# Weights written to SBUF as bf16 by casting transfers of GpSimd, without staging and casts, with another order table

## The chip, the cores and the metric

The kernel runs on one core of a Trainium2 chip. The metric is the device time of one execution in microseconds (us). Executions of one kernel spread by about 1% to either side here, so medians of several runs are given. A ratio is the mean time of one kernel's fast runs over that of the kernel before in the same rounds on the same chip, with a 95% interval, so it is not quite the ratio of the medians quoted beside it. A run over 1.5% above the fastest of the same kernel counts as slow; medians are over all runs, ratios over fast ones alone, and all profiles shown are of fast runs.

The engines are called PE or TensorE (matmuls; PEld its weight loads), DVE or VectorE, ACT or ScalarE, POOL or GpSimd, and SP or SyncE, which here only issues transfers. Operands lie in SBUF and the results of matmuls in PSUM, both memories on the chip. A staging buffer is a place in SBUF where float32 data lands before an engine casts it to bf16.

## The reference, cut to what matters

Sliding-window attention (a query sees keys at a distance up to 32) over 8 batches, 8 heads, 576 positions of 64 values; then a feed-forward part with a 3-tap convolution along the sequence and a sigmoid gate. Input and output are float32.

```python
scores = q @ k.T / 8;  scores[abs(i - j) > 32] = -1e9
x = softmax(scores) @ v                       # 8 x 576 x 512 after joining the heads
h = maximum(x @ w_in, 0)                      # w_in 512 x 1024
c = conv_w[0]*h[s-1] + conv_w[1]*h[s] + conv_w[2]*h[s+1]
out = (h * sigmoid(c)) @ w_out                # w_out 1024 x 512
```

## The kernel before

The kernel is one list of operations. A table, ORDER, gives the order in which they are emitted, the engine of each and its buffers; each engine, SyncE's queue included, runs its share strictly in that order. A token is the number of an operation, a letter (P TensorE, V VectorE, S ScalarE, G GpSimd, D a transfer issued by SyncE, Q one issued by ScalarE, F a matmul on zeros) and buffer numbers.

```python
BUFS = {'st': 3, 'qkb': 5, 'qkT': 3, 'attn': 2, 'rec': 4, 'xn': 3, 'hT0': 8, 'hT1': 6, 'hT2': 6, 'cp': 2, 'gT': 4, 'y': 7}
...
    class InOrder:                        # every engine keeps the order of the table
        def __getattr__(self, name):
            do = getattr(self.engine, name)
            return lambda *args, **kwargs: fixed(do(*args, **kwargs))
...
    def load_v(b, c):                     # v of batch b, block c of 128 keys: rows of 64 floats, 256 bytes each
        ...
            loader[e].dma_start(vst[s0 - lo:s1 - lo, c, :, :], v[b, :, s0:s1, :].rearrange("h p d -> p h d"))
    def shift_v(b, c0, c1):               # vo: v moved by 64 keys, from the bf16 copy ve
        op(f"vo hi {b} {c0} {c1}", lambda e: copy(e, vo[0:64, c0:c1], ve[64:128, c0:c1]), ...)
...
    def load_w(which, i):                 # half a weight, 1 MB of float32, into a buffer of the ring "st"
        s = w_slot[which, i] = Slot(ring)
        ...                               # issued by SyncE (D in the table)
                loader[e].dma_start(
                    flat[:, 0:KC * n].rearrange("p (c f) -> p c f", c=KC),
                    moe_w_in.rearrange("(c p) f -> p c f", p=128)[:, :, n * i:n * i + n])
    def cast_w(which, m):                 # 16 casts, on ScalarE, GpSimd and VectorE
                copy(e, w_in_sb[:, :, 128 * m:128 * m + 128], src[:, :, 128 * (m % n):128 * (m % n) + 128])
```

The ring st holds q and k as they arrive and, in between, the weights. vst holds one float32 batch of v, block by block: the next batch's block can land only when this batch's block has been cast to ve.

The softmax here doesn't subtract the row's maximum and nothing guards it: scores larger than these inputs give would overflow.

## Time and profile before

| | before |
|---|---|
| median, range | 227.55 us, 226.43 to 228.67 (2 runs) |
| span of the profiled run | 225.6 us |
| columns that the real matmuls must stream | 194.2 us |
| first matmul on w_in | 25.80 us |
| TensorE's loss before it / after it | 18.6 / 8.9 us |

"Loss" is the length of a stretch less the columns of the real matmuls that start in it, at one column per 1/2.4 ns. (The prediction adds rounded stretches to 9.1 us; 221.7 - 194.2 - 18.6 is 8.9.) The lines of the page, of the stretches and of the chain stand in the prediction.

### The profile page before, as it was taken

Reading aid. Unit: us, or ns where it says so; the run is one execution under the profiler, and the core shown is the slowest. Engines: PE = TensorE matmul, PEld = TensorE weight load, DVE = VectorE, ACT = ScalarE, POOL = GpSimd, SP = SyncE. Lnnn points to the kernel's source line nnn. Section 1 sums busy time; section 2 is a strip of 40 time slices with the busy share of each in tenths; the row PEclk is TensorE's granted clock in tenths of the full one; section 3 lists DMA queues with packets and bytes.
Section 4 is the critical chain, followed back from the end, with each engine's and each line's share of the span. In section 5 each row is a group of like instructions: output and inputs, shape, how many; then the busy total and the mean of one; then the engine's idle time right before and its main releaser. Section 6 shows DMA issues by size and latency. Waiting matters only on the chain.

```text
span 225.6 us, 7189 instructions
## 1 busy us (share of the span) xinstructions
PE 211.5 (94%) x2720; PEld 122.9 (54%) x2720; DVE 197.3 (87%) x467; ACT 187.5 (83%) x474; POOL 137.7 (61%) x203
## 2 busy tenths in 40 slices
PE   7698899989989999989999998999999999999993
PEld 5366567658555655545555454545655565455541
DVE  6279869899999979797999788989999999899990
ACT  2689899998989889879889989689989999777642
POOL 5978654654376937695368736756386735566640
PEclk9889999999999999999999999999999999999999
DMA  6999999999989999999997989994535212501224
GB/s 201 331 285 358 355 266 281 321 308 253 290 170 324 317 175 287 236 306 224 288 347 129 202 278 358 182 231 147 144 36 118 99 46 49 175 1 49 93 101 178
DMA packets 66391, 48.16 MB, mean 214 GB/s; under 512 B 50781, under 2 KB 50805, under 8 KB 66357
## 3 DMA queue, kind: packets, MB, share of 16 engines
q1 hardware_dynamic: 64992, 46.32, 78.6%
q10 hardware_dynamic: 1364, 1.39, 2.9%
q8 instruction: 21, 0.34, 0.8%
q14 instruction: 14, 0.11, 0.2%
HBM read 32.52 MB, written 9.44 MB: 186 GB/s over the span
## 4 chain that ended last, share of the span: by engine, by line
PE 41%; DVE 18%; ACT 17%; DMA 13%; issue 5%; SPq 3%; POOL 2%; DVEq 0%; ACTq 0%; POOLq 0%
PE pf L232 41%; DMA st<-in_k_dram 7%; ACT attn L232 6%; DVE pf L232 5%; DVE gT L232 4%; SPq L232 3%; DMA out_dram<-y 3%; ACT xn L232 3%; DVE qkT L232 2%; ACT pf L232 2%; DMA vo<-ve 2%; DVE attn L232 2%; DVE xn L232 2%; ACT qkb L232 2%; ACT y L232 1%
## 5 line engine op out<-in xcount | busy, mean ns | idle before, releaser
L232 PE MATMUL pf<-xT,w_in_sb 128*128 128x385 bf16 (+2 forms) x416 | 73.4, 315 | 3.6 <-ACT hT L232 0.9
L232 PE MATMUL pf<-w_out_sb,gT 128*128 128x512 bf16 x288 | 72.2, 380 | 0.0
L232 POOL TENSOR_SCALAR cp<-hT,conv_w_sb 128x384 f32<-128x384 bf16 (+1 forms) x63 | 38.9, 622 | 46.1 <-ACT hT L232 20.2
L232 ACT ACTIVATE pf<-pf 128x384 f32<-128x384 f32 (+1 forms) x104 | 48.2, 477 | 13.1 <-DVE pf L232 11.1
L232 DVE SCALAR_TENSOR_TENSOR gT<-pf,hT 128x384 bf16<-128x384 f32 (+1 forms) x104 | 52.1, 517 | 5.5 <-ACT pf L232 5.1
L232 PEld LDWEIGHTS <-w_in_sb 128*128 128x128 bf16 x416 | 38.6, 98 | 27.8 <-issue 4.5
L232 ACT ACTIVATE attn<-pf 128x512 bf16<-128x512 f32 (+1 forms) x96 | 41.4, 522 | 1.8 <-PE pf L232 1.8
L232 ACT ACTIVATE hT<-pf 128x385 bf16<-128x385 f32 (+2 forms) x76 | 35.4, 487 | 6.0 <-PE pf L232 5.6
L232 PEld LDWEIGHTS <-gT 128*128 128x128 bf16 x288 | 26.0, 98 | 25.7 <-DVE gT L232 0.5
L232 DVE SCALAR_TENSOR_TENSOR pf<-hT,conv_w_sb,pf 128x384 f32<-128x384 bf16 (+1 forms) x61 | 34.7, 586 | 1.2 <-PE pf L232 1.1
L232 PE MATMUL pf<-hT,diag_w 128*128 128x384 bf16 (+1 forms) x153 | 30.9, 309 | 0.9 <-DVE xn L232 0.6
L232 POOL TENSOR_SCALAR qkb<-st 128x1152 bf16<-128x1152 f32 (+1 forms) x23 | 25.7, 1122 | 7.6 <-DMA st<-in_k_dram 3.2
L232 DVE COPY qkT<-pf 128x576 bf16<-128x576 bf16 x35 | 25.6, 750 | 4.9 <-PE pf L232 4.9
L232 POOL TENSOR_TENSOR cp<-cp,cp 128x384 f32<-128x384 f32 (+1 forms) x24 | 24.4, 1016 | 1.6
L232 DVE TENSOR_TENSOR attn<-attn,mask 128x1152 bf16<-128x1152 bf16 x26 | 23.0, 886 | 2.4 <-ACT attn L232 2.3
L232 ACT ACTIVATE xn<-pf,rec 128x64 bf16<-128x64 f32 x96 | 22.0, 360 | 1.5 <-DVE rec L232 1.5
L232 ACT COPY y<-pf 128x512 f32<-128x512 f32 x30 | 18.1, 605 | 3.9 <-PE pf L232 3.7
L232 DVE SCALAR_TENSOR_TENSOR pf<-hT,conv_w_sb,cp 128x384 f32<-128x384 bf16 (+1 forms) x35 | 21.2, 618 | 0.0
L232 POOL TENSOR_TENSOR attn<-attn,mask 128x1152 bf16<-128x1152 bf16 x6 | 14.2, 2371 | 8.4 <-ACT attn L232 8.4
L232 DVE TENSOR_TENSOR xn<-pf,rec 128x256 bf16<-128x256 f32 x48 | 18.9, 410 | 0.0
L232 ACT COPY qkT<-pf 128x576 bf16<-128x576 bf16 x29 | 18.6, 664 | 0.4 <-PE pf L232 0.2
L232 PEld LDWEIGHTS <-diag_w 128*128 128x128 bf16 x153 | 13.3, 97 | 9.8 <-issue 1.3
(49 smaller groups left out, 235.2 us busy)
## 6 DMA issues: line engine op xcount, KB each, us to landing
st<-in_q_dram SPq DMA_DIRECT2D x16, 576.0 KB, 6.8
out_dram<-y SPq DMA_DIRECT2D x36, 256.0 KB, 3.8
st<-in_k_dram SPq DMA_DIRECT2D x14, 576.0 KB, 8.2
vst<-in_v_dram SPq DMA_DIRECT2D x24, 256.0 KB, 7.0
vst<-in_v_dram SPq DMA_DIRECT2D x15, 192.0 KB, 5.7
vo<-ve SPq DMA_DIRECT2D x11, 260.0 KB, 5.6
st<-in_moe_w_in_dram SPq DMA_DIRECT2D x2, 1024.0 KB, 9.3
st<-in_moe_w_out_dram SPq DMA_DIRECT2D x2, 1024.0 KB, 9.4
```

Source lines behind the costliest of these rows:

```text
L232: return lambda *args, **kwargs: fixed(do(*args, **kwargs))
```

## The change

Its intent is to take 16 casts, the staging and its waits away: GpSimd can issue a transfer that converts float32 to bf16 on the way. The rest of the table was made anew for it. The core of the diff (cuts marked; the table, the choice of convolution ways and small index changes are left out):

```diff
-BUFS = {'st': 3, 'qkb': 5, 'qkT': 3, 'attn': 2, 'rec': 4, 'xn': 3, 'hT0': 8, 'hT1': 6, 'hT2': 6, 'cp': 2, 'gT': 4, 'y': 7}
+BUFS = {'st': 3, 'qkb': 4, 'qkT': 3, 'attn': 2, 'rec': 8, 'xn': 2, 'hT0': 9, 'hT1': 7, 'hT2': 7, 'cp': 8, 'gT': 3, 'y': 6}
+MASKS = ('ma', 'mm', 'mm', 'mm', 'mm', 'mm', 'mm', 'am')   # 'a': the mask is added on TensorE
 ...
     def load_w(which, i):
-        s = w_slot[which, i] = Slot(ring)
 ...
-                loader[e].dma_start(
-                    flat[:, 0:KC * n].rearrange("p (c f) -> p c f", c=KC),
+                gpsimd.dma_start(
+                    w_in_sb[:, :, n * i:n * i + n],
 ...
-    def cast_w(which, m):
 ...
-        op(f"cast w_{which} {m}", emit, reads=[("wst", which, m // n)], writes=[("w_" + which, m)], use=[s])
```

In the new table both w_in transfers stand near the front of GpSimd's list, and both w_out transfers behind the first shifts of v. SyncE's order is different too: q and k of both halves of batch 0 come before v block 2.

## The prediction

> **What bounds the kernel now.** I read the engine shares first, then the slices, then cut the span into stages with the view of busy time by stretch, and only then the chain of waits. The page of the kernel before, engine shares and slices (each digit a fortieth of the span, in tenths):
>
> ```profile
> PE 211.5 (94%) x2720; PEld 122.9 (54%) x2720; DVE 197.3 (87%) x467; ACT 187.5 (83%) x474; POOL 137.7 (61%) x203
> ...
> PE   7698899989989999989999998999999999999993
> DVE  6279869899999979797999788989999999899990
> ACT  2689899998989889879889989689989999777642
> ...
> DMA  6999999999989999999997989994535212501224
> ```
>
> TensorE is busy 94% of the span, but two things flatter that: 75 matmuls on a tile of zeros (13.5 us in the list of groups) only keep its clock up, and the end of a matmul is modelled. So I counted what it must do, from the starts and shapes of the matmuls in the trace: all real matmuls stream 194.2 us worth of columns at one column per 1/2.4 ns. The median step between two like matmuls of 512 columns is 216 ns against 213 ns of columns, so this rate is reached. The busy time by stretch (columns: length, then PE, weight loads, DVE, ACT, POOL, clock, DMA share, GB/s):
>
> ```profile
> 0.00:25.80 25.80, 21.13 (x329) 14.52 (x329) 17.43 (x56) 18.53 (x46) 19.67 (x65) 0.93 0.98 298
> 25.80:51.40 25.60, 24.82 (x354) 16.24 (x355) 21.85 (x56) 24.43 (x67) 14.39 (x20) 1.00 1.14 303
> 51.40:103.50 52.10, 49.71 (x808) 29.88 (x805) 48.10 (x115) 45.35 (x112) 34.08 (x34) 1.00 1.07 256
> 103.50:136.20 32.70, 30.87 (x410) 17.10 (x403) 28.87 (x68) 29.71 (x77) 19.04 (x23) 1.00 1.04 257
> 136.20:184.50 48.30, 48.25 (x604) 26.52 (x604) 47.05 (x103) 42.48 (x108) 31.50 (x37) 1.00 0.64 152
> 184.50:221.70 37.20, 36.70 (x228) 18.64 (x226) 33.95 (x74) 26.32 (x67) 19.04 (x26) 1.00 0.24 79
> ```
>
> Against these lengths the columns of real matmuls that start in each stretch are 7.2, 23.9, 49.0, 30.0, 48.3 and 35.7 us. TensorE therefore loses 18.6 us before its first matmul on w_in, then 1.7, 3.1, 2.7, 0.0 and 1.6: 9.1 us in all the rest. The final copy and store add 225.6 - 221.7 = 3.9. So a new order has 9.1 us to win in the middle, plus whatever the start yields; 48 us of the span cannot move. The chain of waits (start, length, what) says who costs these losses:
>
> ```profile
> 1.83 6.50 DMA st<-in_k_dram
> ...
> 16.40 2.95 ACT attn L232 x7
> ...
> 25.80 7.68 PE pf L232 x93
> ...
> 35.45 0.63 ACT w_out_sb L232
> ...
> 38.64 0.50 ACT w_out_sb L232
> 39.14 0.18 ACT attn L232
> 39.32 0.21 ACT w_out_sb L232
> ...
> 136.25 48.21 PE pf L232 x603
> ```
>
> The start is a load, then ScalarE (busy 12.40 of the 12.5 us from 12.5 to 25). From 33.5 to 51 the chain is all ScalarE, with w_out casts on it: 0.63 + 0.50 + 0.21 = 1.34 us. From 51 to 75 it is VectorE. From 136 on TensorE alone.
>
> **What the skill says.** "DMA: Bandwidth & Descriptors", SWDGE vs HWDGE vs iDMA: a transfer that casts must be issued by GpSimd, whose cores write its descriptors; its Latency and other measured facts put first byte at about 1 us against 0.6. No GpSimd transfer is in the trace of before, so this is untested here. The same page, Issuing engines are not separate DMA queues: all queues share the 16 engines. This trace has the DMA share at 0.98 in the first 25.8 us, so an added early transfer takes from the others. "SBUF — State Buffer", Who interferes with whom, says GpSimd is blocked while a VectorE copy uses both ports; descriptors could be late by one VectorE copy, 0.4 to 0.8 us here. "TensorE: Matmul & The Clock Gate", What's actually happening: an idle array runs at half clock. The granted clock here is 0.89 in the first 12.5 us, with 75 zero matmuls to hold it, and 1.00 from 25 on; the page and the trace agree.
>
> **The change, part by part.** (1) Casts of the weights go:
>
> ```profile
> L232 POOL TENSOR_SCALAR w_in_sb<-st 128x512 bf16<-128x512 f32 x4 | 3.3, 836 | 0.6 <-DMA st<-in_moe_w_in_dram 0.5
> L232 ACT CAST w_in_sb<-st 128x512 bf16<-128x512 f32 x4 | 2.6, 771 | 0.0
> L232 ACT CAST w_out_sb<-st 128x512 bf16<-128x512 f32 x4 | 2.5, 621 | 0.0
> L232 POOL TENSOR_SCALAR w_out_sb<-st 128x512 bf16<-128x512 f32 x3 | 1.8, 617 | 3.6 <-DMA st<-in_moe_w_out_dram 3.6
> ```
>
> ScalarE loses 5.1 us (4 x 0.771 = 3.1 and 4 x 0.621 = 2.5 as single durations), POOL 5.1, DVE 0.5. On a path: the 1.34 us shown, and about 1.5 us of the w_in casts on ScalarE, which stand between the exponentials and the normalisation of batch 0 (19.3 to 23.2). In exchange POOL writes four sets of descriptors, an estimate of 4 x 1 us from the skill's 1 us.
>
> (2) The two w_in transfers stand first on POOL after its memsets, with no wait. The memsets end at 2.8 us before; the changed kernel adds seven small ones (affine selects took 0.24 us each), so I expect issue at 4 to 5 us, while k of the first batch lands at 8.4 and its second half at about 12.5. SP now issues q and k of both halves ahead of most of v (0.26 MB, 0.9 us at 298 GB/s earlier). If 2 MB of w_in takes half of the engines from 6 us on, the remaining 1.4 MB at 150 GB/s lands at about 15, 2.5 us later than now. From that landing to the first w_in matmul is 25.8 - 12.5 = 13.3 us now; less 1.5 (casts) and about 1.3 (part 3). 15 + 10.5 = 25.5: the start is a draw, -2 to +3.
>
> (3) Batch 0's second half and batch 7's first are masked by adding -30000 on TensorE: 8 matmuls of 512 columns and 4 of 128, 8 x 0.213 + 4 x 0.053 = 1.9 us more; four VectorE multiplies of 886 ns go, 3.5 us. In batch 0 the exponential then leads straight to the value matmuls: one to two multiplies (0.76 each at 19.4 and 20.9) off the starting chain, so 1.3.
>
> (4) The new tables. Comparing the two programs' instructions: zero matmuls 75 to 16 (none before the second half of batch 0's scores); turning matmuls 58 to 44 (14 x 0.053 = -0.7); taps on TensorE 118 to 123 of 384 and 35 to 24 of 192 (+0.8 - 0.9). With part 3, TensorE has 194.2 + 1.1 = 195.3 us of columns. VectorE, with the durations of before: 18 fewer qkT copies (-13.5), 22 fewer PSUM taps (-13.5), masks -3.5, more casts and copies: about -10 us. ScalarE: 18 more qkT copies (+12.0) against 5.6 of weight casts, 6.3 of q and k casts, 3.6 of y: about -4. POOL: 10 more sums (1.03 each), 14 more 384-column products (0.62 each), with the rest about +17, to 155, still the least busy. cp goes from 2 buffers to 8, rec 4 to 8, hT one more of each; xn 3 to 2, gT 4 to 3, y 7 to 6, qkb 5 to 4.
>
> The sum from the profiled 225.6: start 0; middle, 9.1 us of losses cut by some 4.5 (1.34 from w_out casts; the VectorE stretch from 51 to 75 shorter; products waiting for a cp buffer, 17.0 us of POOL waits on DVE in the table of waits, mostly off the path); TensorE work +1.1; end 0. That is -3.4, or 222 in the profile. The plain time is 227.55 beside it, so some 224. I go 1.7 us lower, to 222.3, by choice: an order table that comes with a change was presumably searched until it paid, and that belief, not a profile line, is the reason.
>
> **Rivals.** The start gets worse: w_in collides with q and k, and without zero matmuls TensorE is cold. For it: DMA share 0.98, clock 0.93 even with them. Against: half speed costs only about 0.5 us per batch of 18 to 36 small matmuls (0.44 to 1.14 us each at full speed), and w_in was needed before the same first matmul anyway. It would make 226 to 229. Second rival: TensorE is the bound and the casts were hidden; only the 1.1 us of new columns show, 227 to 229. For it: the 48 us stretch without loss. Against: ScalarE and VectorE saturated from 33 to 75. Third: fewer buffers of xn, gT and qkb make new waits on loads and batches, taking back what the casts gave: 224 to 227. Fourth, a good one: the losses of the middle fall under 3 us and the start gains 2: 217 to 219.
>
> **Range and chances.** The best case and the bad start give 217 and 227.5 as the eight-in-ten range. Two per cent is 4.55 us, so the border lies at 223.0, just above my number: faster 0.53, same 0.41, slower 0.06.
>
> **What would show it.** First w_in matmul at 24 to 28 us; k of batch 0's second half landing near 15; clock below 0.9 in the first 25 us; a POOL-issued queue of 4 MB read; ScalarE near 183 and VectorE near 187 us busy; the stretches between first w_in matmul and 136 us losing 4 instead of 7.5 us. I am wrong if the first w_in matmul comes after 29 us, if w_out lands so late that the first w_out matmuls wait, or if the middle loses as much as before.

## More of the kernel before

One more view is needed for later: what SyncE issued between 23 and 37 us, from its timeline (start and length in us; the length is that of issuing).

```profile
23.34 0.37 SPq L232 DMA_DIRECT2D st<-in_moe_w_out_dram  x1
23.76 3.51 SPq L232 DMA_DIRECT2D vst<-in_v_dram  x2
27.39 4.15 SPq L232 DMA_DIRECT2D st<-in_moe_w_out_dram  x1
31.58 5.42 SPq L232 DMA_DIRECT2D vst<-in_v_dram  x4
```

SyncE's queue never stands still here: weights and small v blocks follow one another in one queue.

## The result, and the profile after

238.20 us (237.87 to 238.53, 2 runs) against 227.55: ratio 1.047 [1.038, 1.057], slower. The range of the prediction ended at 227.5.

The page of the changed kernel, engine shares and slices in tenths:

```profile
PE 205.2 (87%) x2653; PEld 116.8 (49%) x2653; DVE 199.6 (84%) x462; ACT 185.1 (78%) x474; POOL 160.5 (68%) x224
...
PE   1325796897999999999999899989999999999992
...
PEclk9999999999999999999999999999999999999998
DMA  6999989956898999999999989999503712430324
```

PE is thin up to about 59 us (ten slices of 5.9 us) and full after that. DMA dips to 5 and 6 in slices 9 and 10, where it was full before. The clock line reads full from the start, but that is no measurement: this trace has no record of the clock before 23.37 us, and the view prints a stretch without a record as full. The matmuls tell otherwise. The first 18 small turning matmuls of the attention, in the changed kernel and, at a clock recorded as full, before:

```profile
6.45 0.84 PE L233 MATMUL pf<-ident,qkb 64*128 64x64 bf16 x18 [1.21 <-DVE qkb L233]
```

```profile
7.09 0.44 PE L232 MATMUL pf<-ident,qkb 64*128 64x64 bf16 x18 [0.48 <-POOL qkb L232]
```

So without the zero matmuls TensorE ran at about half speed here. (Before, too: its first clock record is at 6.29 us, and up to then its zero matmuls of 256 columns started 213 ns apart, against 109 ns at full clock. The 0.89 that the prediction reads for the first 12.5 us is therefore too high.) Busy time by stretch (columns as in the prediction; the clock of 1.00 in the first line is the missing record):

```profile
0.00:31.35 31.35, 13.55 (x276) 9.23 (x277) 19.81 (x67) 14.21 (x32) 19.23 (x63) 1.00 0.95 241
31.35:62.50 31.15, 26.18 (x375) 16.25 (x377) 23.56 (x59) 25.84 (x72) 12.04 (x17) 1.00 0.82 181
62.50:103.00 40.50, 39.25 (x598) 23.43 (x596) 37.38 (x92) 36.37 (x98) 29.45 (x31) 1.00 1.02 273
```

The first stretch ends at the first matmul on w_in, 31.35 us. Counted as before, TensorE loses 23.1 us in the first stretch (18.6 before), 7.1 in the second (1.7 before, up to 51.4), and 6.5 in all the rest up to 232.0 (7.2 before). The columns are 195.3 us (+1.1), the tail 4.4 (3.9). So 4.5 + 5.4 - 0.7 + 1.1 + 0.5 = 10.8 us, the whole difference between the two spans: 9.9 of it are waits in the first 62 us, and the later table loses even 0.7 us less. The chain of waits says what made it (start, length, what):

```profile
3.37 15.02 DMA vst<-in_v_dram
18.41 0.63 ACT ve L233
...
20.81 2.56 DVE diag_w L233 x6
...
31.20 0.35 DVE ve L233
31.57 0.47 SPq L233
...
32.13 8.20 DMA vst<-in_v_dram
```

There are two barriers, that is, waits for a load behind which the engines come to stand, one after the other. **The first**: v block 2 of batch 0 is issued at 3.37 us and lands at 18.38, after 15.0 us. Before, it was issued at 2.34 and landed at 9.36. ScalarE waits 4.09 us for it, in its fixed order, while other work stands behind; VectorE and TensorE follow. w_in had been issued at 4.44 and 5.39 and landed at 14.70 and 18.06, long before its first use at 31.35. With w_in moved away and SyncE's order kept (x2 below) the same block landed at 12.41. So of the 9.0 us by which it is later than before, about 3 come from its new place behind q and k of the second half, and about 6 from w_in beside it. **The second**: SyncE is idle for 8 us. Its timeline, to be laid beside the one of before:

```profile
22.55 0.90 SPq L233 DMA_DIRECT2D st<-in_k_dram  x1
31.57 0.47 SPq L233 DMA_DIRECT2D vo<-ve  x1
32.13 9.44 SPq L233 DMA_DIRECT2D vst<-in_v_dram  x5
```

The shift vo<-ve waits for a VectorE cast that ends at 31.5, and the v block behind it, which has nothing to do with that cast, is issued only at 32.13. It then takes 8.2 us, because GpSimd's two w_out transfers (issued at 29.12 and 29.91) are in the same 16 DMA engines. VectorE waits for it with relu and gate behind.

Why so long for a small block? In the trace a v block is some 64 packets of 256 bytes on each DMA engine, 20 to 23 ns each: 1.4 us of work. The Trainium skill, "DMA: Bandwidth & Descriptors", Queues, rings and completion order, says that an engine goes round robin between the queue rows it has work for. The first barrier agrees: from 12 to 16 us 609 packets of v and 603 of GpSimd's casting packets (1024 bytes written) started, of 31 and 96 ns on average. At one for one, 64 x (31 + 96) ns is 8.1 us, an estimate from these durations; the packets of v run from 9.7 us, and the block landed at 18.38. (The page speaks of turns of some 9 to 17 descriptors; these counts cannot tell turns of one record from turns of several.)

The second barrier is not the same. Between 30.71 and 36.14 us no packet of SyncE's queue started at all, only GpSimd's, although the shift had been issued at 31.57 and the v block at 32.13; v's own packets then took from about 37.2 to 40.4 us. Why SyncE's queue stood still there is not shown. Before, weights and v stood in one queue, where a v block waits only for what was issued ahead of it.

### The profile page after: what moved, and what is told of

Its sections match the earlier page's. It is cut to its first block, busy times and chain, and to the rows that moved or that the text cites. A ratio compares the mean times of both kernels' runs of the same rounds, so it can differ in the third digit from the quotient of the medians.

```text
span 236.4 us, 7025 instructions
## 1 busy us (share of the span) xinstructions
PE 205.2 (87%) x2653; PEld 116.8 (49%) x2653; DVE 199.6 (84%) x462; ACT 185.1 (78%) x474; POOL 160.5 (68%) x224
## 4 chain that ended last, share of the span: by engine, by line
PE 35%; DVE 28%; DMA 12%; POOL 9%; ACT 7%; issue 5%; SPq 2%; DVEq 0%; ACTq 0%; POOLq 0%
PE pf L233 35%; DMA vst<-in_v_dram 10%; DVE pf L233 9%; POOL cp L233 6%; DVE gT L233 5%; ACT attn L233 3%; DMA xT<-xn 2%; DVE hT L233 2%; DVE qkT L233 2%; ACT pf L233 2%; DVE xn L233 2%; SPq L233 2%; DVE attn L233 1%; DVE y L233 1%; DVE diag_w L233 1%
## 5 line engine op out<-in xcount | busy, mean ns | idle before, releaser
L233 POOL TENSOR_SCALAR cp<-hT,conv_w_sb 128x384 f32<-128x384 bf16 (+1 forms) x84 | 58.5, 706 | 33.2 <-DVE hT L233 17.1
L233 ACT ACTIVATE pf<-pf 128x384 f32<-128x384 f32 (+1 forms) x104 | 46.4, 468 | 13.5 <-DVE pf L233 9.8
L233 PEld LDWEIGHTS <-w_in_sb 128*128 128x128 bf16 x416 | 38.2, 98 | 25.9 <-issue 3.2
L233 POOL TENSOR_TENSOR cp<-cp,cp 128x384 f32<-128x384 f32 (+1 forms) x37 | 36.2, 985 | 1.3
L233 ACT COPY qkT<-pf 128x576 bf16<-128x576 bf16 x47 | 28.9, 657 | 9.5 <-PE pf L233 9.3
L233 ACT ACTIVATE hT<-pf 128x385 bf16<-128x385 f32 (+2 forms) x72 | 32.7, 485 | 4.6 <-PE pf L233 2.9
L233 PE MATMUL pf<-hT,diag_w 128*128 128x384 bf16 (+1 forms) x147 | 30.7, 313 | 4.1 <-DVE hT L233 3.2
L233 DVE SCALAR_TENSOR_TENSOR pf<-hT,conv_w_sb,cp 128x384 f32<-128x384 bf16 (+1 forms) x41 | 29.3, 728 | 3.1 <-POOL cp L233 2.6
L233 DVE SCALAR_TENSOR_TENSOR pf<-hT,conv_w_sb,pf 128x384 f32<-128x384 bf16 (+1 forms) x40 | 22.7, 571 | 4.5 <-PE pf L233 4.3
L233 PE MATMUL pf<-ident,qkb 64*128 64x64 bf16 x576 | 15.1, 196 | 10.2 <-ACT qkb L233 5.2
L233 POOL TENSOR_SCALAR qkb<-st 128x1152 bf16<-128x1152 f32 (+1 forms) x18 | 21.5, 1203 | 2.7 <-DMA st<-in_q_dram 1.4
L233 DVE TENSOR_TENSOR attn<-attn,mask 128x1152 bf16<-128x1152 bf16 x22 | 20.4, 925 | 0.1
L233 PEld LDWEIGHTS <-qkb 64*128 64x128 bf16 x576 | 11.2, 98 | 17.1 <-DVE qkb L233 9.1
```

## The experiments

Eighteen runs were made, in five rounds. Milestones below are from one profile each: "w_in" is the first matmul on w_in, "gate n" the start of the n-th gate operation on VectorE. Profiles of kernels that share an order up to some point differ there by up to 1.6 us, so a single milestone is no finer than that.

| run | median us | ratio [95%] | w_in | gate 4 | gate 12 | gate 32 |
|---|---|---|---|---|---|---|
| before | 227.55 | | 25.8 | 32.7 | 46.7 | 83.1 |
| after | 238.20 | 1.047 [1.038, 1.057] | 31.4 | 43.9 | 56.0 | 92.9 |
| x1_old_order_cast_dma | 233.31 | 1.024 [1.015, 1.033] | 26.4 | 33.6 | 47.4 | 85.3 |
| x2_w_in_later | 240.31 | 1.056 [1.051, 1.062] | 29.1 | 44.0 | 57.4 | 94.4 |
| x3_v_earlier | 240.44 | 1.058 [1.050, 1.067] | 31.1 | 44.1 | 58.3 | 95.2 |
| x6_zero_matmuls | 240.04 | 1.056 [1.050, 1.062] | 32.6 | 44.3 | 56.3 | 93.3 |
| x7_vo_on_vector | 236.83 | 1.034 [1.025, 1.043] | 30.9 | 40.5 | 52.6 | 89.5 |
| x4_w_out_later | 238.85 | 1.046 [1.036, 1.055] | 30.7 | 40.4 | 53.0 | 89.9 |
| x5_all_four | 234.06 | 1.021 [1.014, 1.028] | 28.7 | 38.3 | 52.3 | 89.4 |
| x9_w_from_scalar | 234.29 | 1.019 [1.009, 1.029] | 30.5 | 37.6 | 51.4 | 88.0 |
| x10_no_casts (wrong) | 230.62 | 1.008 [1.001, 1.014] | 26.0 | 32.9 | 46.4 | 86.0 |
| x11_only_w_out | 228.14 | 1.005 [0.998, 1.013] | 25.1 | 32.0 | 45.8 | 83.6 |
| x13_batch1_first | 233.50 | 1.026 [1.022, 1.030] | 28.5 | 38.5 | 50.5 | 87.6 |
| x15_diag_on_gpsimd | 232.90 | 1.025 [1.020, 1.030] | 27.8 | 37.8 | 49.8 | 86.7 |
| x16_batch3_first | 233.77 | 1.027 [1.021, 1.033] | 28.2 | 39.3 | 51.4 | 88.3 |
| x17_half_weights_after (wrong) | 233.28 | 1.027 [1.021, 1.033] | 29.1 | 38.7 | 50.8 | 87.7 |
| x18_half_weights_before (wrong) | 234.43 | 1.030 [1.024, 1.036] | 26.1 | 33.0 | 48.9 | 85.6 |
| x19_stores_later | 227.79 | 1.002 [0.996, 1.008] | 26.2 | 33.1 | 47.0 | 82.6 |
| x20_v_before_products | 232.24 | 1.021 [1.013, 1.028] | 28.6 | 39.3 | 50.1 | 87.0 |
| x21_w_out_and_stores | 228.69 | 1.004 [0.997, 1.011] | 25.9 | 32.8 | 46.7 | 83.5 |

Edits of the table are written with the names of the operations.

### Round one: which part of the change, and the start

**x1_old_order_cast_dma**: the old table and buffers; only the way of the weights is new.

```diff
 # old table; at the places of SyncE's weight loads
-  loader[e].dma_start(flat..., moe_w_in...)    # SyncE, into the ring
+  gpsimd.dma_start(w_in_sb..., moe_w_in...)    # casting, and the same for w_out
   cast_w: emit nothing
```

> The headline part alone: the order table of before, with w_in and w_out written as bf16 by casting transfers from GpSimd at the places where SP loaded them, and no weight casts. If casting transfers cost time by themselves (descriptors, slower transfers, shared engines), this is slower than before, 229 to 233 us. If what cost 10.7 us was where the transfers and loads stand in the new order, this is as fast as before or 1 to 3 us faster (224.5 to 227.5), the first w_in matmul at 24 to 26 us, ScalarE 5 us less busy.

233.31, 1.024 [1.015, 1.033]. About half of the loss is there with the old table: without a single cast of weights the kernel is slower than with them. It is 0.6 us late at the first w_in matmul and 2.2 at gate 32.

**x2_w_in_later**, **x3_v_earlier** and **x6_zero_matmuls** change one thing of the start of the new table each.

```diff
 x2:  GpSimd:  -load w_in 0, load w_in 1 (ahead of diag 4)   +behind cast q 0 1 4 9
 x3:  SyncE:   -load v 0 2 behind load k 0 1                 +ahead of load q 0 1
 x6:  TensorE: +61 zero matmuls in the gaps of the start, as the old table had
```

> The changed kernel with the two w_in transfers moved on GpSimd from right behind the memsets (issued at 4.4 and 5.4 us) to behind its cast of q of the first batch (about 14 us). Theory A (the early 2 MB push the v load of column block 2 from about 13.5 to 18.4 us, and ScalarE, VectorE and then TensorE stand behind it in their fixed order): that v load lands at 13.5 to 15, the first w_in matmul comes at 26.5 to 28.5 instead of 31.35, the time falls by 3 to 6 us to 232 to 235. Rival B (the new order of SP's loads is to blame, not the transfers): the v load still lands after 17 us, less than 1.5 us gained.

> The changed kernel with the v load of column block 2 issued before q and k of the second half, as before had it; w_in still first on GpSimd. If the blocked cast of that v block is what holds the start, the v load lands at 8 to 10 us, ScalarE's 4.1 us wait for it goes, and the first w_in matmul comes at 27 to 29.5: 2 to 4 us gained, also with the early w_in. If the early w_in delays the whole start whatever stands in line (k then lands at 15 or later), less than 1.5 us gained.

> The changed kernel with 61 more matmuls on zeros in the gaps before batch 0's second half, as before had them. Theory C (a cold TensorE made the start late): the first w_in matmul comes 1 to 3 us earlier and the time falls by as much. Theories A and B: the gaps are waits for loads, so less than 0.6 us changes either way.

None gained time: 240.31, 240.44, 240.04, with intervals that overlap that of the changed kernel. The zero matmuls brought nothing (first w_in matmul at 32.6), and the chain of the changed kernel has no piece of TensorE before 24.52 us; so there is no sign that the cold TensorE held the start. It is not a full test: x6 itself has half clock on record from 21.0 to 27.8 us. w_in later did bring the first w_in matmul to 29.10, as the first barrier demands, and yet gate 4 stood at 44.0 to 44.3 in all three, as in the changed kernel (43.9). The second barrier took the gain: in x2 SyncE issued the v block of batch 1 at 29.96 and it landed at 40.39, as late as before the move. x3 moved one v block ahead, and the next one (issued at 5.66, landed at 20.55) took its place on the chain. Both traces also have 6.8 us of half clock on record, from 40.3 us in x2 and 42.6 in x3, which the changed kernel does not have; part of what they are slower than it may be that.

### Round two: the second barrier, and both together

```diff
 x7:  -vo hi 1 1 2 (SyncE)                      +vo hi 1 1 2 (VectorE, behind cast v 1 1)
 x4:  GpSimd: -load w_out 0, load w_out 1       +both behind vo hi 1 0 1
 x5:  the moves of x2, x3, x7 and x4 together
 x9:  old table, casts kept; the four weight loads D (SyncE) -> Q (ScalarE)
```

> The changed kernel, but the first shift of v of batch 1 (vo<-ve, block 1) is a VectorE copy right behind the cast that it waits for, instead of a DMA in SyncE's fixed order. In the changed kernel SyncE sat idle from 23.5 to 31.57 us behind that DMA and the v block behind it landed at about 40.3. Theory (second barrier: a wait in SyncE's queue plus the w_out transfers of GpSimd): the v block is issued near 24 and lands before 31, the fourth gate comes at 38 to 40 instead of 43.9, and the time falls by 3 to 5 us to 233-235. Rival (the order of the later part pins the end, or VectorE, which gets 0.5 us more work, is the bound): the fourth gate comes earlier but the end stays, 237 to 240.

> The changed kernel, but the two w_out transfers stand two shifts of v later on GpSimd, so that they start at about 36 to 41 us instead of 29 and do not share the DMA engines with the v block that is issued at 32. Theory (packets of the GpSimd ring halve the pace of the small v packets): that v block lands in about 4 us instead of 8.2, the fourth gate comes at 39 to 41 instead of 43.9 and the time falls by 1 to 4 us to 234-237, unless the first w_out matmuls then wait. Rival (only the late issue by SyncE counts, not the shared engines): the block still takes over 7 us, and the time stays at 238 to 240.

> The changed kernel with four moves together: w_in issued behind the last cast of q of batch 0 on GpSimd, v block 2 of batch 0 loaded before q and k of the second half, the shift of v of batch 1 on VectorE, w_out two shifts later. Theory (two barriers in series, each made by a GpSimd transfer and a load in a fixed order; one alone is absorbed by the other): first w_in matmul at 27 to 29.5, fourth gate at 34 to 37, time 228 to 232, a gain larger than the sum of the single ones. Rival (the delay is in the casting transfers or the late-stage order themselves): 235 or more.

> The kernel before, staging buffers and casts kept, but the four weight loads are issued by ScalarE's queue instead of SyncE's, at the same places of the table. Theory (a second ring takes half the packets of every engine and delays the small loads of SyncE; casting and GpSimd have no part in it): about as slow as the old table with GpSimd's casting transfers would be without the removed casts, 231 to 236, with v blocks of 8 us and more beside weight transfers. Rival (GpSimd's descriptors or the casting itself are what is slow): within 2 us of the kernel before, 226 to 230. ScalarE's own issue time, an estimate of 4 times 0.6 us from the issues of 0.6 us seen on it, is in both.

x7: gate 4 at 40.5 and 236.83; in the profile about as expected (3.4 us), in time less (1.034 against 1.047, with intervals that touch). x4 is the clean test of shared DMA engines: the same v block, issued at 31.52 instead of 32.13, landed after 3.0 us instead of 8.2 once the w_out transfers were not beside it, and gate 4 came 3.5 us earlier. The time did not follow: the transfers, now at 36 us, met the v blocks issued there, which took 9.7 and 11.1 us. So either half of the barrier can be lifted, but w_out, moved, delayed other v blocks instead. x5 lifted both barriers: first w_in matmul 28.7, gate 4 at 38.3, 234.06, ratio 1.021. That is the first clear gain over the changed kernel, though short of the expected 228 to 232.

x9 is inconclusive. It was to separate "another queue" from "casting". But ScalarE came to the w_in loads only at 13.19, behind exponentials, 4.5 us later than SyncE had, and the first w_in matmul moved by 4.7, so the late issue is enough to explain that. Half clock is on record in it from 24.1 to 30.9 us besides.

### Round three: what the casts were worth

**x10_no_casts**: the old table, plain loads by SyncE, and no cast of weights at all: TensorE reads the upper two bytes of each float.

```diff
-  w_in_sb = sb.tile([128, KC, d_ff], BF16)
+  w_in_f = sb.tile([128, KC, d_ff // 2], FP32)
+  w_in_sb = w_in_f.bitcast(BF16).rearrange("p c (f h) -> p c f h", h=2)[:, :, :, 1]   # and w_out alike
   load_w: half 0 into w_in_f, half 1 into its old staging buffer, not used;  cast_w: emit nothing
   matmuls: block m -> m % 4, so that half 0 is used twice
```

> The kernel before with its own table, in which no engine casts the weights and GpSimd moves nothing either: SyncE loads the weights plainly at the same places, and TensorE takes the upper two bytes of each float (every second bf16 of the tile). To fit, only the first half of either weight is used and the second load goes to its old staging buffer, so the result is wrong on purpose. It is the old table with casting transfers with only the way of the weights exchanged. Theory (the removed casts are worth 1 to 4 us, and the casting transfers from a second ring cost 6 us and more): 224 to 227, at least 5 us faster than the old table with casting transfers (233.3). Rival (removing the casts shifts the engines' pace so that the loads collide, whoever issues them): 231 to 235. If the matmuls with every second element are slower, their durations in the trace show it (216 ns per 512 columns now) and the test says less.

230.62, 1.008 [1.001, 1.014]: no gain. But the time says less than that, for the reason that the expectation names: a matmul of 512 columns on w_out, which here streams every second bf16, starts 226 to 227 ns after the one before it instead of 216 (288 of them: up to 3 us more for TensorE); those on w_in took 315 ns in both. So a gain of up to 3 us could be hidden in the time. The milestones are better up to 62.8 us, where only some 30 of these matmuls (0.3 us) have run: w_in 26.0 against 25.8, gate 12 at 46.4 against 46.7, gate 24 at 62.8 in both. ScalarE had 3.0 us less to do (184.5 against 187.5) and waited for others instead. In the start, the chain of x10 runs through VectorE from 19.7 to 25.9 us. Then 3 us are lost at one place. GpSimd's timeline in x10:

```profile
77.61 1.15 POOL L229 TENSOR_SCALAR qkb<-st 128x1152 bf16<-128x1152 f32 x1 [3.09 <-DMA st<-in_q_dram]
```

and in the kernel before:

```profile
74.41 1.15 POOL L232 TENSOR_SCALAR qkb<-st 128x1152 bf16<-128x1152 f32 x1
```

Up to there the milestones of the two traces agree within 0.4 us; then a load of q, issued 1 us later, lands too late, and the rest stays 3 to 4 us behind. Why it landed this late is not settled; one profile cannot tell it from the spread of DMA times.

**x11_only_w_out**, with **x13_batch1_first** and **x15_diag_on_gpsimd** from the other side:

```diff
 x11: old table; only w_out by gpsimd.dma_start(w_out_sb...), its 8 casts gone; w_in as before
 x13: x5, but w_out at its own place, and SyncE: load v 1 4, load v 1 3 ahead of load v 2 0
 x15: x13, and diag 5, diag 7: VectorE -> GpSimd, behind cast k 1 0 0 9
```

> The kernel before with its own table, w_in as before (plain loads, casts on ScalarE and GpSimd); only w_out comes by two casting transfers of GpSimd, at the places of SyncE's loads, and its eight casts are gone. Theory (a casting transfer from a second ring delays SyncE's loads whenever the DMA engines are full, and they are full up to 150 us): about half of the loss of the old table with both, so 229 to 232. Rival (only w_in, in the start, is harmful; w_out is needed late and its 1.34 us of casts stood on the chain): 225 to 228, faster than before.

> The changed kernel with w_in behind the last cast of q of batch 0, v block 2 of batch 0 early, the shift of v of batch 1 on VectorE as in the four moves together, w_out in its own place, and in addition the last two v blocks of batch 1 ahead of v of batch 2 in SyncE's order, because in the run of the four moves SyncE sat idle from 24.9 to 33.8 us behind a v block of batch 2 that had no free buffer. Theory (what is left against before is idle time of SyncE's queue in 24 to 37 us, which the full DMA engines cannot make good): fourth gate at 36 to 38, twelfth gate at 48 to 50 instead of 52.3, time 229 to 232. Rival (the pace of the engines in the later part of the table sets it): twelfth gate at 52, time 234 and more.

> As the one with batch 1 first, and in addition the two triples of diagonal weights that VectorE makes at 17.5 to 20 us (2.5 us on the chain of the start) are made by GpSimd once it has cast k of batch 1. Theory (the rest of the late start is VectorE's order): first w_in matmul at 25.5 to 27 instead of 28.7, time another 1 to 2.5 us less. Rival (w_in itself, landing at 24.6, or another engine then holds the start): first w_in matmul after 28, no change of time.

x11: 228.14, 1.005 [0.998, 1.013]. w_out by casting transfers in the old table is neither gain nor loss, though its casts stood on the chain of waits; no matmul is slower in it. By difference, if the two halves simply add, the loss of x1 comes with w_in; its milestones show no single place for it. x13 and x15 moved their milestones the way that was expected, but just short of the ranges (x13: gate 4 at 38.5, gate 12 at 50.5; x15: w_in 27.8), and their times, 233.50 and 232.90, cannot be told from x5.

### Round four: is DMA work the bound?

At this point the traces showed a regularity. Count as DMA work the packets finished by 70 us, each with the median duration of its size and kind of queue in these traces, over 16 engines: 61.5 us before, 54.9 after. That plus the time of gate 32 (83.1 and 92.9) lies between 144.6 and 148.7 in all fourteen traces up to here. The theory then was that the DMA engines are a second bound of the first 85 us.

```diff
 x16: x15, and SyncE: load q 3 0, load k 3 0 ahead of load v 2 4 (and of the first transposing transfer)
 x17: the changed kernel; load_w: if i == 1: return (half the bytes; matmuls use half 0 twice)
 x18: x10; load_w: if i == 1: return
 x19: old table; store 0 1, 0 0, 1 0, 0 2 behind load k 4 1 on SyncE
```

> As the kernel with the diagonals on GpSimd, and in addition q and k of the first half of batch 3 are loaded ahead of the last v block of batch 2 and of the first transposing transfer, because their staging buffer is free from about 31 us and SyncE sat idle from 47.4 to 51 us in front of that transfer. Theory (DMA work done by 70 us sets the 32nd gate, and idle time of SyncE's queue is what is lost): DMA work at 60 us rises from 54.3 to 56-58, the 32nd gate comes at 84 to 86 instead of 86.7, time 230 to 232. Rival (the engines' own order in the new table sets the pace): 32nd gate at 86.7 or later and 232.5 to 235 however early the loads are.

> The changed kernel with only the first half of w_in and of w_out moved (the other half of the matmuls uses the same half again, so the result is wrong on purpose). 6.7 us of work of all DMA engines goes, 3.3 in the start and 3.3 near 30 us, and nothing else. Theory (the DMA engines are a bound of the first 85 us): first w_in matmul at 28 to 29.5 instead of 31.35, 32nd gate at 86 to 89 instead of 92.9, time 231 to 235. Rival (only the order and the engines' waits matter): 237 to 240.

> The kernel before without casts and with the upper halves of the floats (230.6 in its run), and in addition without the second half of w_in and of w_out; wrong on purpose. 6.2 us of DMA work less by 37 us. Theory (DMA engines a bound of the first 85 us): 32nd gate at 80 to 83 instead of 86.0, time 225 to 228. Rival (TensorE with VectorE and ScalarE set the pace there): 32nd gate at 85 to 86.5, time 229 to 231.5.

> The kernel before, correct, with its four first stores of results moved behind the loads of q and k of batch 4 in SyncE's order; a free y buffer is not needed before 98 us. Theory (DMA work of loads is a bound there): q and k of batch 4 land about 2 us earlier (k at 78 instead of 80.3), the 32nd gate comes 0.5 to 2 us earlier, time 226 to 227.8, 0 to 1% faster than before. Rival (TensorE alone bounds it): no change within 0.3%.

The theory fell: x18 has 6.2 us less DMA work than x10, and its gate 32 came at 85.6 against 86.0, where 80 to 83 was expected. (The sum is 140.3 in x18 and 140.1 in x17, outside the old range.) On the way it lost 2.5 us to x10 between gates 8 and 12, and won them back where x10 waits for its load of q. VectorE's timeline of x18 there:

```profile
44.41 1.86 DVE L229 COPY vo<-ve 64x520 bf16<-64x520 bf16 x2
46.29 1.26 DVE L229 CAST ve<-vst 128x512 bf16<-128x512 f32 x1
```

The same three instructions in x10:

```profile
44.35 0.61 DVE L229 COPY vo<-ve 64x520 bf16<-64x520 bf16 x2
44.99 0.43 DVE L229 CAST ve<-vst 128x512 bf16<-128x512 f32 x1
```

And GpSimd in x18 at that time:

```profile
44.93 2.34 POOL L229 TENSOR_SCALAR qkb<-st 128x1152 bf16<-128x1152 f32 x2
```

In x10 GpSimd waited from 44.2 to 45.4 for v and cast k only at 48.33. In x18 the loads came earlier, so GpSimd cast q and k just while VectorE copied in SBUF, and VectorE's 1.04 us became 3.1. The Trainium skill, "SBUF — State Buffer", Who interferes with whom, says that GpSimd shares a port pair with VectorE and that the one who comes second blocks. The trace agrees. So earlier loads made a new collision, and the constant sum does not show a cause. That x18 was also slower in the end, 1.030 [1.024, 1.036], is another matter: in its trace the loss against x10 falls between gates 64 and 80 (124.8 to 157.5 us against 124.4 to 154.7), where TensorE waits for a v block that lands at 138.74 and then has half clock on record for 3.4 us from 140.7, busy all the time.

x17 gained as much as all of x5's moves: 1.027 [1.021, 1.033], with nothing but half of the weight bytes taken away, and all its milestones fell in the expected ranges. So half of the weight bytes account for about 2 of the 4.7 points in the new table; whether by the bytes or by where they collide, it does not tell. x16 gained nothing: 233.77, gate 32 at 88.3, as its rival said. x19 brought gate 32 forward by 0.5 us and the time not at all, 1.002.

### Round five: the rest of the new table, and a version that beats both

GpSimd in x15, from its timeline, after the last shifts that it could do early:

```profile
34.70 1.31 POOL L230 TENSOR_SCALAR vo<-ve 64x520 bf16<-64x520 bf16 x2 [0.37 <-DVE ve L230]
43.30 1.85 POOL L230 TENSOR_SCALAR cp<-hT,conv_w_sb 128x192 f32<-128x192 bf16 x3 [7.29 <-ACT hT L230]
45.12 0.62 POOL L230 TENSOR_SCALAR ve<-vst 128x512 bf16<-128x512 f32 x1
...
46.23 1.71 POOL L230 TENSOR_SCALAR vo<-ve 64x520 bf16<-64x520 bf16 x2
```

It waits 7.29 us for the input of a product, while a cast of v whose data has landed stands behind in the fixed order; then it does all of it in a row, and TensorE is busy only 3.71 of the 5 us from 45 to 50. A similar row of work stands in the changed kernel, at 49.5 to 55.2.

```diff
 x20: x15, and GpSimd: cast v 1 3, vo hi 1 3 4 ahead of cp 1 2 0 0
 x21: x11 and x19 together
```

> The kernel with the diagonals on GpSimd (232.9), and in addition the cast of v block 3 of batch 1 and one shift of it stand before the first products on GpSimd, where it was idle from 36 to 43.3 us; 1.2 us leave its chain from 43.3 to 49.5. Theory (that chain holds TensorE from 45 to 55): the 12th gate unchanged near 49.8, exponential 25 and the 32nd gate 1 to 1.5 us earlier (63 and 85.5), time 231 to 232.3. Rival (the chain is not what holds, or another wait takes its place): 32nd gate at 86.5 or later, time 232.5 to 234.

> The kernel before with both edits that cost nothing: w_out by casting transfers of GpSimd without casts on the engines (228.1, 1.005), and the four first stores behind the loads of batch 4 (227.8, 1.002). The first was 0.7 us ahead in its profile until 60 us and lost it at 70 to 83, where the second gains. Theory (both gains add): 225.5 to 227, ratio 0.990 to 0.998. Rival (each change of pace meets other waits): 227.5 to 229.5.

x20: from gate 4 to gate 12 took 10.8 us instead of 12.0, the expected gain, but its start was later by 1.5 us at gate 4 for no reason in the edit, and its time of 232.24 (1.021 [1.013, 1.028]) cannot be told from x15. x21: 228.69, 1.004 [0.997, 1.011], no gain. No version beat the kernel before.

## Why the prediction was wrong, point by point

**What bounds the kernel** was read rightly for the last two thirds: TensorE alone, and the changed kernel loses little there. For the first third I counted TensorE's losses but did not ask what SyncE's queue and the DMA share of about 1 meant for the pace of the loads. Of the clock I took a stretch without a record for a full one.

**Part (1), casts**: the sizes were right (ScalarE 185.1 against "near 183"; four issues of 0.94, 0.75, 0.79 and 0.75 us against an estimate of four times 1). Their worth was wrong. I took 1.34 us of w_out casts and 1.5 of w_in casts for time on a path because the chain of waits named them. With all casts gone and the weights still loaded by SyncE (x10) no milestone up to 62.8 us came earlier by more than 0.4 us, and w_out without casts (x11) gained nothing. The chain shows one way back through the trace; that others of nearly the same length stood beside it is the likely reason (in x10 ScalarE waited for others instead), not one that a run isolates.

**Part (2), the start**: this step failed first. I named the collision but put it on q and k and sized it by sharing bandwidth: "the remaining 1.4 MB at 150 GB/s lands at about 15". k landed at 13.04. It was v, whose small packets now took turns with GpSimd's large ones: 15.0 us instead of 7.0, and landed 9.0 us later, 6 of them by w_in and 3 by the new order. "-2 to +3" was +5.5 (25.80 to 31.35).

**Part (3), masks on TensorE**: the columns rose by 1.1, as worked out. Its gain in the start cannot be seen behind the wait for v.

**Part (4), the tables**: "VectorE about -10 us" was +2.3 (199.6 against 197.3). I multiplied counts by the durations of before, but these depend on what GpSimd does at the same time. The taps that VectorE adds to GpSimd's products, in the list of groups of before:

```profile
L232 DVE SCALAR_TENSOR_TENSOR pf<-hT,conv_w_sb,cp 128x384 f32<-128x384 bf16 (+1 forms) x35 | 21.2, 618 | 0.0
```

and after:

```profile
L233 DVE SCALAR_TENSOR_TENSOR pf<-hT,conv_w_sb,cp 128x384 f32<-128x384 bf16 (+1 forms) x41 | 29.3, 728 | 3.1 <-POOL cp L233 2.6
```

Split by what GpSimd did, those of 384 columns after took 619 ns (12 of them) where GpSimd ran for less than half of their time and 786 ns (24), with up to 1269, where it ran for more. Taps whose second operand is in PSUM took 620 and 616 ns, split the same way. This is the same page's rule that two SBUF inputs contend with GpSimd. GpSimd had 23 us more to do (160.5 against 137.7). Over all VectorE instructions, the time above each form's fast duration (its tenth percentile) rose from 9 to 18 us. That is most of why the estimate of VectorE failed; it is not what made the kernel slow, since after 62 us nothing more was lost.

**The sum**: "middle, 9.1 us of losses cut by some 4.5" failed. From the first w_in matmul to 137 us the loss is 7.1 + 2.8 + 1.8 = 11.7 us instead of the 4 that I named. The term that was not in the sum at all is the 8 us in which SyncE stood before a transfer that waits for VectorE. I compared counts and durations of the two tables, not the order of SyncE's list against the events it waits for.

**By choice**: the 1.7 us taken off because a table that comes with a change "was presumably searched until it paid" had no line behind it, and the belief was wrong.

**Rivals**: "the start gets worse: w_in collides with q and k" was the right one in kind; its 226 to 229 was too small, since it left the second barrier out. Of cold TensorE the fact was right (0.84 us for 18 small matmuls that took 0.44 before), but no run shows that it cost time: no TensorE stands on the chain before 24.52 us, and adding zero matmuls (x6) did nothing. My sign for it, a clock below 0.9 in the view, could not have shown it.

**Shown and open.** Shown: the small v loads beside casting transfers (x4: 8.2 to 3.0 us), the serial barriers (x2 and x3 alone nothing, x5 with both 1.021), the share of half of the weight bytes (x17, about 2 of the 4.7 points) and that the casts were worth next to nothing up to 62.8 us (x10) and those of w_out nothing in the time (x11). Argued, not shown: what held SyncE's queue from 31.6 to 36.1 us in the second barrier. Open: the other half of the loss. Every repaired form of the new table stays 2.1 to 2.7% over before. In the profile of x15 TensorE loses 5.6 us from 37 to 62 us, against 2.5 before; GpSimd's row of work may be one piece of that, by x20's stretch, but no run's time tells the pieces apart. Also open is why w_in by casting transfers costs the old table more (x1) than plain loads without casts (x10).

## What to carry to other kernels

An operation named by the chain of waits is worth its time only if nothing else ends at nearly the same moment; take it away in an experiment before counting it. A transfer moved to another queue no longer waits in line: here it took turns with the small loads of the first queue or held them up, and one transfer in a fixed-order queue that waits for an engine holds up every load behind it. Less work is not less waiting: earlier loads in x18 made two engines collide. And before a clock is read as full, see whether the trace has a record of it there; the steps between like matmuls are the check.

## What the Trainium skill lacked or had wrong

- "DMA: Bandwidth & Descriptors", Queues, rings and completion order: the page gives packets of about 9 to 17 descriptors. It lacks what round robin does to small loads: from 12 to 16 us 609 packets of 256 bytes started beside 603 of 1024 bytes written, so the small ones moved at the pace of the large. Nor does it tell of a queue standing still beside another: in the second barrier SyncE's first packet started 4.6 us after its issue (31.57 to 36.14), and a v block took 8.2 us, 3.0 without w_out beside it.
- The same page, SWDGE vs HWDGE vs iDMA: no figure is given there for the engine time of a casting transfer. Here w_in, 1 MB written (2 MB read), took 1024 packets of 97 ns on average, much like the 2048-byte packets of the plain load (100 ns, 982 counted from 4 to 20 us), so the cast itself cost the DMA engines next to nothing; the issues cost GpSimd 0.75 to 0.94 us each.
- "SBUF — State Buffer", Who interferes with whom: right, but without sizes for these instructions, which here were 0.30 to 0.93 us for a copy, 0.43 to 1.26 for a cast, and 619 to 786 ns on average for a tap with two SBUF inputs.
